# Attention's quarter blocks put next to each other, low words moved to VectorE, and another order at the head of the last layer

## The chip, the cores and the metric

The kernel runs on one core of a Trainium2 chip. The metric is the device time of one execution in microseconds (us), as the median of three runs. TensorE (PE) does the matmuls, VectorE (DVE), ScalarE (ACT) and GpSimd (POOL) the elementwise work, and SyncE (SP) issues nearly all the transfers.

## What is computed

Three layers follow each other. Attention is elementwise sigmoid attention over 4 batches of 12 heads, 448 tokens each, 64 wide. A router then assigns each of the 1792 tokens to one of 8 experts, by sorted preference and with a cap of 224, and each expert is a two-matmul block. A dense layer with a squared ReLU ends it.

```python
scores = scale * np.matmul(q, k.transpose(0, 1, 3, 2)) - np.log(S)
attn = 1.0 / (1.0 + np.exp(-scores)); x = np.matmul(attn, v)     # attention
out[mask] = np.maximum(x[mask] @ w1[e], 0.0) @ w2[e]             # per expert e
r = np.maximum(x @ w_in, 0.0); y = (s * (r * r) + b) @ w_out     # dense layer
```

Inputs are float32 (the dense layer's weights come as float64). Where full precision is wanted, a float32 operand is split in two words: a high word rounded to the matmul's format, and a low word that is the rest. Three matmuls of such words make one product.

## The kernel before

**Attention.** Heads come in pairs, pairs in groups of two. A group q (0 to 11) has seven blocks of scores: three blocks of 128 keys for each pair, and block 3, which holds the last 64 keys of both pairs. Block 3 is the two quarter blocks of the group: each of its matmuls uses a quarter of the array (64 rows, 64 columns), and four of them run at once, one in each quarter. The product with the values has the same shape there. The other score blocks use the array as two halves of 64 rows (two matmuls at once), the other value blocks as two halves of 64 columns.

The loop at line 453 runs over the groups. An iteration q has two halves. In a half, `split_qk` (line 277) splits one pair of q and k of group q + 2 on VectorE (lines 282 and 283); `values` (line 320) multiplies half of group q; `scores` (line 289) computes blocks of group q + 1; then `convert` turns one block of the dense layer's float64 weights to float32 on VectorE (lines 152 to 157) and issues its store (line 147) and the next load (line 141). The first half computes score blocks 0 to 2, the second blocks 3 to 6. In the second half `values` begins with the quarter blocks (line 328) and goes on with three full blocks (line 334). A sigmoid on ScalarE (line 313) takes a block of scores from PSUM to an `attn` tile; there are three PSUM buffers for scores.

At the top of an iteration SyncE issues the loads of two pairs of q and k (`load_qk`, lines 273 and 274) and of the values of group q + 2 (`load_v`, line 268). All of these and the conversions' transfers stand in SyncE's one queue in the order of the program, so that a load at the top of iteration q stands behind the transfers of the conversions of iteration q - 1. The values have three buffers; those of groups 0 and 1 are loaded ahead of the loop.

Every third iteration opens a batch (q = 3, 6, 9). It also computes the router's logits of the batch before: a matmul block in the first half (`gate`, line 354), and in the second half a turn of the logits (line 366), a copy to the tile L on ScalarE (line 376), and ranks on VectorE (`prefs`, lines 380 to 383). In the last batch, `bracket` takes the range of the logits in three stages (0 on VectorE, 1 with the matmul of line 393, 2 with that of line 401), each followed by small VectorE work.

In the last iterations the first four weight blocks of the experts are made ready: a transfer (`w_dma`), a high word on ScalarE (`w_high`, line 244) and at once its low word on GpSimd (`w_low(G)`, line 254). When attention ends, `prefs` of the last batch opens the router, a chain of small steps that go from engine to engine.

**Head of the last layer.** The dense layer's first product is done as a scheme of seven half-width products for each of 8 pairs of column blocks. `layer_mixed` (line 1125) writes out their order by hand as a list of (f, m): f is the block, m the product. A product is nine matmuls of 448 columns. Product (f, 3) accumulates in the same PSUM bank as (f, 5) and has to come after VectorE has taken (f, 5) out of it (line 1194). The weight blocks come in a list of units with an order of its own (line 218), and the products take them in that order; the copies of results go to scratch tiles chosen by the list `picks` (line 1146).

Of the kernel before, what the change touches and what calls it, by code (L numbers as in the profile page):

```python
# [8 lines left out]
F32 = mybir.dt.float32  # L9
# [10 lines left out]
B, H, S, D = 4, 12, 448, 64  # L20
# [26 lines left out]
NQ = B * NP // 2  # L47
# [18 lines left out]
def tile_kernel(ctx, tc, qT, kT, v, wg, w1, w2, wi, wo, s2, b2, cst, out):  # L66
    nc = tc.nc
    V, A, G, T = nc.vector, nc.scalar, nc.gpsimd, nc.tensor
# [55 lines left out]
    vp = att.enter_context(tc.tile_pool(name="vp", bufs=2))  # L124
    at = att.enter_context(tc.tile_pool(name="at", bufs=2))
# [33 lines left out]
    def convert():  # L159
        if not coming:  # L160
            return
        i = coming.pop(0)
        a = cgp.tile([128, 768], I32, name="co", bufs=3)
        b = cgp.tile([128, 768], I32, name="cb_", bufs=1)
        r = craw.pop(i)
        for step in range(3):
            to_float(a, b, r, step)
        if i < KG // 2:
            V.tensor_scalar(a, a, -(1 << 31), None, op0=ALU.bitwise_xor)
        cout.append((i, a))  # L170
        cv_out(1)
        cv_in()
# [33 lines left out]
    nu = {"dma": 0, "high": 0, "low": 0, "use": 0, "ahead": 5}  # L206
# [5 lines left out]
    for g in range(4):  # L212
        for e in (2 * g, 2 * g + 1):
            units += [w1[e, f] for f in range(KF)] + [w2[e, n] for n in range(KF)]
            where += [False] * (2 * KF)
        more = [narrow[f] for f in range(KG)] if g < 2 else []
        if g == 3:
            more = [(0, 1), (1, 1), (2, 1), (0, 2), (1, 2), (0, 3), (1, 3), (0, 4), (1, 4), (2, 2), (2, 3)]
            for f in range(3, KG // 2):
                more += [(f, 1), (f - 1, 4), (f, 2), (f, 3)]  # L220
            more += [(KG // 2 - 1, 4)]
        if g % 2:
            more += [w for of in products for w in of]
        units += more
        where += [False] * len(more)
# [22 lines left out]
    def w_low(eng=None):  # L248
        i = nu["low"]
        if i < nu["high"]:  # L250
            r, h = w_source(i), splits[i]
            lo = wlp.tile([128, KD, 128], F32R, name="wl")[:, :r.shape[1]]
            eng = eng or (G if where[i] else V)
            eng.tensor_sub(lo, r, h.bitcast(F32))  # L254
            splits[i] = (h, lo)
            nu["low"] += 1
# [6 lines left out]
    raw_qk, two_qk, vt, attn, pvs, plg, lgs, pts = {}, {}, {}, {}, {}, {}, {}, {}  # L263
    pairs = [(b, p) for b in range(B) for p in range(NP)]

    def load_v(q):
        vt[q] = vp.tile([128, 7, 128], F32, name="vt", bufs=3)
        nc.sync.dma_start(vt[q], v[q // 3, q % 3])

    def load_qk(i):  # L270
# [18 lines left out]
    def scores(q, units):  # L289
        if q >= NQ:  # L290
            return
        for r in units:
            p = ps_s.tile([128, 2, 512], F32, name="psc")
            if r == 3:
                work = [(2 * q + n, slice(HD, S), slice(n * 64, n * 64 + 64)) for n in range(2)]
            else:
                c = r % 4
                work = [(2 * q + r // 4, slice(c * 128, (c + 1) * 128), slice(0, 128))]
            plain = q < PLAIN or r == 3
            n_terms = 1 if plain else 3  # L300
            for m in range(n_terms):
                for j in range(2):
                    me = slice(j * D, (j + 1) * D)
                    for n, keys, rows in work:
                        if plain:
                            kx = qx = raw_qk[n]
                        else:
                            h, lo = two_qk[n]
                            kx, qx = ((h, h), (lo, h), (h, lo))[m]
                        T.matmul(p[rows, j, :S], kx[me, 1, keys], qx[me, 0], start=(m == 0),  # L310
                                 stop=(m == n_terms - 1), skip_group_check=True)
            attn[q, r] = at.tile([128, 2, S], F32, name="attn", bufs=7)
            A.activation(attn[q, r], p[:, :, :S], AF.Sigmoid, bias=nls, scale=1.0 / math.sqrt(D))  # L313
        if units[-1] == 6:
            for n in (2 * q, 2 * q + 1):
                raw_qk.pop(n)
                if q >= PLAIN:
                    two_qk.pop(n)
# [42 lines left out]
    def gate_turn(b, stop):  # L361
        lg = lgs.pop(b)
        pt = small_psum()
        pts[b] = pt[:CP, :NC * E].rearrange("p (c e) -> p c e", e=E)
        for c in range(NC):
            T.matmul(pts[b][:, c], lg[:, c * CP:(c + 1) * CP], ct[:, C_SEL:C_SEL + E], start=(c == 0),
                     stop=(stop and c == NC - 1))
# [18 lines left out]
    def bracket(stage):  # L386
        if stage == 0:
            lv = L[:, :NCH - NC].rearrange("p c e -> p (c e)")
            V.tensor_reduce(mm[:CP, 0:1], lv, axis=AX.X, op=ALU.max)
            V.tensor_reduce(mm[:CP, 1:2], lv, axis=AX.X, op=ALU.min, negate=True)  # L390
        elif stage == 1:
            pm = small_psum()
            T.transpose(pm[:2, :CP], mm[:CP], ident[:CP, :CP])
            m2 = ep.tile([2, 1], F32, name="m2")
            mt = ep.tile([2, CP], F32, name="mt")
            A.copy(mt, pm[:2, :CP])
            V.tensor_reduce(m2, mt, axis=AX.X, op=ALU.max)
            V.tensor_scalar(dg, ident[:2, :2], m2, None, op0=ALU.mult)
        else:
            pr = small_psum()  # L400
            T.matmul(pr[:, :2], on[:2], dg, start=True, stop=True)
            A.copy(mm, pr[:, :2])
            lb = ep.tile([128, 1], BF16, name="lb")
            V.tensor_add(mm[:, 0:1], mm[:, 0:1], mm[:, 1:2])
            V.scalar_tensor_tensor(lb, mm[:, 0:1], -MARGIN, mm[:, 1:2], op0=ALU.mult, op1=ALU.subtract)
            V.tensor_scalar(mm[:, 0:1], mm[:, 0:1], 1.77 * (1 + MARGIN) / LEVELS, None, op0=ALU.mult)
            V.tensor_scalar(mm[:, 0:1].bitcast(I32), mm[:, 0:1].bitcast(I32), 0x7F800000, None, op0=ALU.bitwise_and)
            V.tensor_scalar(least, mm[:, 0:1], LEVELS ** -7.0, None, op0=ALU.mult)
            V.tensor_copy(dv[0][:, 0:1], lb)
            V.tensor_copy(dv[0][:, 1:], mm[:, 0:1].to_broadcast([128, LEVELS]))  # L410
            V.tensor_scalar(th, kvec, dv[0][:, 1:2], dv[0][:, 0:1], op0=ALU.mult, op1=ALU.add)
# [18 lines left out]
    load_qk(2)  # L430
    load_qk(3)
    cv_in()
    load_v(1)
    cv_in()
    cv_in()
    scores(0, range(7))
# [16 lines left out]
    for q in range(NQ):  # L453
        b, t = divmod(q, 3)
        closing = b == B - 1
        for n in (2 * q + 5, 2 * q + 6):
            if n < 2 * NQ:
                load_qk(n)
        if q + 2 < NQ:
            load_v(q + 2)  # L460
        for half in range(2):
            if q + 2 < NQ:
                split_qk(2 * q + 4 + half)
            values(q, half)
            if t == 0 and b:
                if half:
                    gate_turn(b - 1, True)
                    prefs(b - 1)
                else:
                    gate(b - 1, 0, NP, NP)  # L470
                    gate_copy(b - 1)
            if closing and (t == 1 or t + half == 1):
                bracket(2 * t + half - 1)
            if closing and t == 2 and not half:
                gate(b, 0, NP - 2, NP - 2)
                gate_copy(b)
            scores(q + 1, range(3, 7) if half else range(3))
            n = 2 * (NQ - q) - half
            if 2 < n <= 6:
                w_dma()  # L480
            for _ in range({4: 1, 3: 1, 2: 2}.get(n, 0)):
                w_high()
                w_low(G)
            for _ in range(CONV[2 * q + half]):
                convert()
    gate_turn(B - 1, False)
    gate_last(B - 1)
    prefs(B - 1)
# [636 lines left out]
    def layer_mixed(y):  # L1125
        mov["b11"], mov["b21"] = y[:, :HK], y[:, HK:]
        half = slice(CAP, S)
# [15 lines left out]
        rest = [lambda: V.tensor_sub(mov["t4"][:, :, 1], srcs["t4"], mov["t4"][:, :, 0].bitcast(F32))]  # L1143
        tmps = [pool["y"].tile([128, S], F32, name="tmp", bufs=pool["tmp"]) for _ in range(3)]
        tmps += [late["rb"][:, n * S:(n + 1) * S] for n in range(3)]
        picks = [tmps[n] for n in (0, 1, 2, 3, 4, 5, 0, 1, 2, 3, 5)]
        tmps = [tmps[n] for n in (4, 0, 1, 2, 3, 5)]
        gn = gt[:, :, :, 64:64 + S]
        got, bank, tmp, held = {}, {}, {}, []
# [15 lines left out]
        def product(f, m):  # L1165
# [35 lines left out]
            if held and (f, m) in ((0, 7), (1, 7), (0, 6)):  # L1201
# [2 lines left out]
        nu["ahead"] = 4  # L1204
        n = KG // 2
        order = [(0, 1), (0, 2), (1, 1), (1, 2), (2, 1), (2, 2), (0, 7), (1, 7), (0, 6), (1, 6), (0, 4), (0, 5), (1, 4),
                 (0, 3), (1, 5), (1, 3), (2, 7), (2, 6), (2, 4), (2, 5)]
        for f in range(3, n - 1):
            order += [(f, 1), (f, 2), (f - 1, 3), (f, 7), (f, 6), (f, 4), (f, 5)]
        order += [(n - 1, 1), (n - 2, 3)] + [(n - 1, m) for m in (7, 6, 2, 5, 4, 3)]  # L1210
# [118 lines left out]
```

## Time and profile before

| what | value |
|---|---|
| median of three runs | 876.88 us (876.16 to 878.23) |
| the profiled execution's own time | 876.09 us |
| its span, from the first to the last instruction | 874.3 us |
| around the span | 1.8 us |
| PE busy | 857.2 us (98%) |
| DVE busy | 645.3 us (74%) |
| ACT busy | 509.9 us (58%) |
| POOL busy | 92.9 us (11%) |

The span is read in stretches: attention lasts until about 147 us, the router until about 184 us, the experts and the dense layer fill the rest. PE is busy nearly everywhere, so time is won or lost only where PE waits, where its matmuls are spaced wider than they need to be, or in the router's chain, where small steps wait for each other.

### The profile page before, as it was taken

What the parts mean: (1) busy time and instruction counts of PE and PEld (TensorE: products, weight loads), DVE (VectorE), ACT (ScalarE), POOL (GpSimd) and SP (SyncE); (2) the same over time, 40 slices, a digit from 0 to 9 for tenths busy, and PEclk for the clock granted to TensorE, in tenths of its full rate; (3) what the DMA queues carried; (4) which work ended last, traced back from release to release, by engine and by line L of the source; (5) the groups of instructions that cost most, each with busy time, mean ns of one, the idle gap of its engine ahead of it and who ended that gap; (6) DMA issues with size and microseconds to landing.
All of it is one profiled execution on the core that took longest, in us unless ns stands there. A gap on an engine that the chain in (4) does not pass through costs nothing.

```text
span 874.3 us, 14225 instructions
## 1 busy us (share of the span) xinstructions
PE 857.2 (98%) x5188; PEld 740.3 (85%) x5188; DVE 645.3 (74%) x1109; ACT 509.9 (58%) x887; POOL 92.9 (11%) x150
## 2 busy tenths in 40 slices
PE   9999999789999999999999999999999999999997
PEld 4444445579989999999999999999998999999997
DVE  2998979747778786789777957867897666866781
ACT  6666667736655576644665546766675555655440
POOL 1000003231000000000445330000000000000003
PEclk9999999969999999999999999999999999999999
DMA  8899995937669775668899986756743423333313
GB/s 307 312 335 363 352 346 178 288 94 263 217 200 324 252 262 178 220 209 297 282 330 323 284 250 206 250 191 202 230 144 106 127 90 118 119 99 95 104 35 131
DMA packets 76778, 190.40 MB, mean 218 GB/s; under 512 B 9120, under 2 KB 31136, under 8 KB 76448
## 3 DMA queue, kind: packets, MB, share of 16 engines
q1 hardware_dynamic: 68800, 164.28, 55.9%
q0 software_dynamic: 7904, 25.17, 10.2%
q8 instruction: 42, 0.69, 0.3%
q14 instruction: 32, 0.26, 0.1%
HBM read 161.11 MB, written 42.47 MB: 233 GB/s over the span
## 4 chain that ended last, share of the span: by engine, by line
PE 89%; DVE 5%; DMA 2%; ACT 1%; issue 1%; POOL 0%; POOLq 0%; DVEq 0%; ACTq 0%; SPq 0%
PE acc L757 15%; PE acc L758 7%; PE acc L1069 7%; PE acc L1072 7%; PE acc L1071 7%; PE psc L310 6%; PE pv L334 5%; PE acc L914 4%; PE acc L915 4%; PE acc L916 4%; PE acc L1178 4%; PE acc L1180 4%; PE acc L1179 4%; PE acc L783 1%; PE acc L784 1%; PE acc L785 1%
## 5 line engine op out<-in xcount | busy, mean ns | idle before, releaser
L244 ACT CAST wh<-raw 128x768 fp32r<-128x768 f32 (+1 forms) x248 | 201.2, 823 | 91.7 <-issue 66.5
L254 DVE TENSOR_TENSOR wl<-raw,wh 128x768 fp32r<-128x768 f32 (+1 forms) x244 | 225.8, 937 | 18.0 <-PE acc L1071 11.0
L757 PE MATMUL acc<-u,wh 128*128 128x448 f32 x384 | 120.8, 374 | 0.0
L758 PE MATMUL acc<-u,wl 128*128 128x224 f32 x384 | 101.6, 265 | 0.2 <-DVE wl L254 0.2
L757 PE MATMUL acc<-x,wh 128*128 128x448 f32 x288 | 94.9, 384 | 0.6 <-issue 0.6
L313 ACT ACTIVATE attn<-psc,nls 128x896 f32<-128x896 f32 x84 | 78.1, 1009 | 23.5 <-PE psc L310 23.4
L758 PE MATMUL acc<-x,wl 128*128 128x224 f32 x288 | 76.9, 267 | 0.0
L757 PEld LDWEIGHTS acc<-u,wh 128*128 128x128 f32 x384 | 72.1, 188 | 5.3
L758 PEld LDWEIGHTS acc<-u,wl 128*128 128x128 f32 x384 | 73.3, 191 | 0.4 <-DVE wl L254 0.4
L914 PE MATMUL acc<-y,wh 128*128 128x448 f32 x192 | 71.0, 370 | 0.7 <-ACT y L772 0.7
L915 PE MATMUL acc<-y,wh 128*128 128x448 f32 x192 | 70.3, 366 | 0.0
L916 PE MATMUL acc<-y,wl 128*128 128x448 f32 x192 | 70.2, 366 | 0.0
L762 ACT COPY tmp<-acc 128x224 f32<-128x224 f32 x96 | 32.9, 343 | 50.1 <-PE acc L758 49.8
L334 PE MATMUL pv<-attn,vt 128*64 128x448 f32 x288 | 59.4, 548 | 0.0
L757 PEld LDWEIGHTS acc<-x,wh 128*128 128x128 f32 x288 | 54.9, 191 | 4.8 <-issue 0.9
L1069 PE MATMUL acc<-wh,as 128*128 128x384 f32 x168 | 56.1, 334 | 0.0
L1071 PE MATMUL acc<-wl,as 128*128 128x384 f32 x168 | 56.1, 334 | 0.0
L1072 PE MATMUL acc<-wh,as 128*128 128x384 f32 x168 | 56.1, 334 | 0.0
L758 PEld LDWEIGHTS acc<-x,wl 128*128 128x128 f32 x288 | 55.8, 194 | 0.3 <-DVE wl L254 0.3
L763 DVE TENSOR_TENSOR tmp<-acc,tmp 128x224 f32<-128x224 f32 x78 | 30.1, 385 | 28.2 <-ACT tmp L762 27.9
L334 PEld LDWEIGHTS pv<-attn,vt 128*64 128x64 f32 x288 | 18.5, 136 | 34.8 <-issue 33.9
L648 POOL DMA_INDIRECT xr<-xs,idx x16 | 16.1, 1008 | 264.9 <-PE px L748 251.9
(339 smaller groups left out, 1985.8 us busy)
## 6 DMA issues: line engine op xcount, KB each, us to landing
raw<-in_w_dram SPq DMA_DIRECT2D x128, 384.0 KB, 3.7
raw<-nw SPq DMA_DIRECT2D x64, 384.0 KB, 3.7
craw<-in_wi_dram SPq DMA_DIRECT2D x16, 768.0 KB, 7.3
raw<-mx SPq DMA_DIRECT2D x32, 384.0 KB, 4.9
nw<-co SPq DMA_DIRECT2D x24, 384.0 KB, 7.5
craw<-in_wo_dram SPq DMA_DIRECT2D x8, 768.0 KB, 7.2
ra<-in_wo_dram SPq DMA_DIRECT2D x8, 768.0 KB, 5.1
hs<-nw POOLq DMA_DIRECT2D x16, 384.0 KB, 9.9
```

Source lines behind the costliest of these rows:

```text
L244: A.copy(h, r)
L254: eng.tensor_sub(lo, r, h.bitcast(F32))
L313: A.activation(attn[q, r], p[:, :, :S], AF.Sigmoid, bias=nls, scale=1.0 / math.sqrt(D))
L334: T.matmul(pv[j * 64:(j + 1) * 64, :S], v[:, 4 * block + c, j * D:(j + 1) * D], a[:, j], start=(block == 0 and c == 0), stop=(block == 1 a ...
L757: T.matmul(p[:, :2 * CAP], wh, src[:, k].rearrange("p a s -> p (a s)"), start=(k == 0), stop=False)
L758: T.matmul(p[:, :CAP], wl, src[:, k, 0], start=False, stop=(k == n - 1))
L914: T.matmul(p, wh, src[:, k, 0], start=first, stop=False)
L915: T.matmul(p, wh, src[:, k, 1], start=False, stop=False)
L916: T.matmul(p, wl, src[:, k, 0], start=False, stop=last)
L1069: T.matmul(acc, hi, wh[:, cols], start=(opens[j] and u == 0 and c == 0), stop=False, skip_group_check=True)
L1071: T.matmul(acc, hi, wl[:, cols], start=False, stop=False, skip_group_check=True)
L1072: T.matmul(acc, lo, wh[:, cols], start=False, stop=(u == 3 and c == 1), skip_group_check=True)
```

## The change

- In an iteration of attention the first half now computes score blocks 0 to 3 and the second blocks 4 to 6. So block 3 of group q + 1 is the last thing that TensorE does in the first half, and the quarter blocks of the values of group q are the first in the second. The `attn` tiles have 8 buffers instead of 7.
- The values have 2 buffers instead of 3. The load of group 1 ahead of the loop is taken out, and iteration q loads the values of group q + 1 instead of q + 2, at the same place in SyncE's queue.
- Stages 1 and 2 of `bracket` come half an iteration later.
- The low words of the first four weight blocks are made on VectorE instead of GpSimd, after the conversion of that half.
- At the head of the last layer product (2, 7) comes ahead of (1, 3), which stood right behind (1, 5); the units (2, 2) and (1, 4) change places, and so do two entries of `picks`.

```diff
-            more = [(0, 1), (1, 1), (2, 1), (0, 2), (1, 2), (0, 3), (1, 3), (0, 4), (1, 4), (2, 2), (2, 3)]
+            more = [(0, 1), (1, 1), (2, 1), (0, 2), (1, 2), (0, 3), (1, 3), (0, 4), (2, 2), (1, 4), (2, 3)]
...
-        vt[q] = vp.tile([128, 7, 128], F32, name="vt", bufs=3)
+        vt[q] = vp.tile([128, 7, 128], F32, name="vt", bufs=2)
...
-            attn[q, r] = at.tile([128, 2, S], F32, name="attn", bufs=7)
+            attn[q, r] = at.tile([128, 2, S], F32, name="attn", bufs=8)
...
     cv_in()
-    load_v(1)
     cv_in()
...
-        if q + 2 < NQ:
-            load_v(q + 2)
+        if q + 1 < NQ:
+            load_v(q + 1)
...
-            if closing and (t == 1 or t + half == 1):
-                bracket(2 * t + half - 1)
+            if closing and 1 <= 2 * t + half <= 4 and 2 * t + half != 2:
+                bracket((2 * t + half) // 2)
...
-            scores(q + 1, range(3, 7) if half else range(3))
+            scores(q + 1, range(4, 7) if half else range(4))
...
                 w_high()
-                w_low(G)
             for _ in range(CONV[2 * q + half]):
                 convert()
+            while nu["low"] < nu["high"]:
+                w_low()
...
-        picks = [tmps[n] for n in (0, 1, 2, 3, 4, 5, 0, 1, 2, 3, 5)]
+        picks = [tmps[n] for n in (0, 1, 2, 3, 4, 5, 0, 1, 3, 2, 5)]
...
-                 (0, 3), (1, 5), (1, 3), (2, 7), (2, 6), (2, 4), (2, 5)]
+                 (0, 3), (1, 5), (2, 7), (1, 3), (2, 6), (2, 4), (2, 5)]
```

## Rows read from the trace of the kernel before

**Rows 1.** Busy time by engine, 75 to 100 us; after POOL: granted clock, DMA share, GB/s
```profile
75.00:100.00 25.00, 25.00 (x184) 11.67 (x180) 21.44 (x32) 16.16 (x21) 0.00 (x0) 1.00 0.96 353
```
**Rows 2.** Timeline of PE, one plain iteration (q = 8): start, duration, engine, line, work
```profile
102.39 2.48 PE L334 MATMUL pv<-attn,vt 128*64 128x448 f32 x12
104.80 0.47 PE L310 MATMUL psc<-wh 64*128 64x448 f32 x2
...
106.81 0.98 PE L328 MATMUL pv<-attn,vt 64*64 64x448 f32 x8
107.73 2.48 PE L334 MATMUL pv<-attn,vt 128*64 128x448 f32 x12
110.13 0.98 PE L310 MATMUL psc<-rqk 64*64 64x448 f32 x8
...
113.14 0.60 PE L334 MATMUL pv<-attn,vt 128*64 128x448 f32 x2
```
**Rows 3.** Timeline of PE: iterations 1, 10 and 11 begin; the matmul of line 393
```profile
22.08 1.35 PE L334 MATMUL pv<-attn,vt 128*64 128x448 f32 x6
...
126.39 2.48 PE L334 MATMUL pv<-attn,vt 128*64 128x448 f32 x12
129.17 0.26 PE L393 MATMUL psc<-ident,mm 112*2 112x112 f32 x1 [0.31 <-DVE mm L390]
138.01 2.48 PE L334 MATMUL pv<-attn,vt 128*64 128x448 f32 x12
```
**Rows 4.** Timeline of SyncE's queue: value loads issued in iterations 0, 2, 5, 7
```profile
19.43 0.96 SPq L268 DMA_DIRECT2D vt<-in_v_dram  x1
...
42.12 0.64 SPq L268 DMA_DIRECT2D vt<-in_v_dram  x1
...
77.39 0.66 SPq L268 DMA_DIRECT2D vt<-in_v_dram  x1
...
99.12 0.42 SPq L268 DMA_DIRECT2D vt<-in_v_dram  x1
```
**Rows 5.** DMA issues, the same four loads: KB, us from issue to landing
```profile
vt<-in_v_dram SPq DMA_DIRECT2D x1, 448.0 KB, 6.7
vt<-in_v_dram SPq DMA_DIRECT2D x1, 448.0 KB, 7.5
vt<-in_v_dram SPq DMA_DIRECT2D x1, 448.0 KB, 7.7
vt<-in_v_dram SPq DMA_DIRECT2D x1, 448.0 KB, 7.2
```
**Rows 6.** Timelines of ACT and DVE: L copied (iteration 3), ranks begin (iterations 3, 6)
```profile
53.95 0.19 ACT L376 COPY L<-psc 112x32 f32<-112x32 f32 x1 [0.34 <-PE psc L366]
...
59.11 0.42 DVE L380 TENSOR_TENSOR ge<-L 112x256 f32<-112x256 f32 x1
...
93.72 0.42 DVE L380 TENSOR_TENSOR ge<-L 112x256 f32<-112x256 f32 x1
```
**Rows 7.** Timelines of DVE, POOL and ACT at the end of attention
```profile
139.72 0.96 DVE L157 CUSTOM_DVE_ANT_0 co<-co,cb__1657 128x1536 uint16<-128x1536 uint16 x1
140.65 6.75 POOL L254 TENSOR_TENSOR wl<-raw,wh 128x768 fp32r<-128x768 f32 x3 [4.88 <-ACT wh L244]
145.77 2.45 DVE L157 CUSTOM_DVE_ANT_0 co<-co,cb__1686 128x1536 uint16<-128x1536 uint16 x1
147.19 0.19 ACT L376 COPY L<-psc 112x32 f32<-112x32 f32 x1 [1.85 <-PE psc L372]
148.14 0.41 DVE L380 TENSOR_TENSOR ge<-L 112x256 f32<-112x256 f32 x1
```
**Rows 8.** Timeline of PE, head of the last layer: the first matmul of product (1, 3)
```profile
676.10 0.44 PE L1178 MATMUL acc<-x,wh 128*128 128x448 f32 x1 [1.75 <-DVE rb L1194]
```
**Rows 9.** Busy time by engine around the router's end, columns as in rows 1
```profile
177.50:191.00 13.50, 11.49 (x47) 8.45 (x47) 2.94 (x11) 1.76 (x4) 4.01 (x4) 0.50 0.38 107
191.00:200.00 9.00, 9.00 (x61) 8.63 (x60) 6.97 (x15) 7.38 (x16) 5.20 (x16) 1.00 0.43 152
```

## Prediction

> **What bounds the kernel now.** I read the busy time by stretches first. In attention PE has no idle time that counts, VectorE is at 86% and the DMA engines at 96% [rows 1]: three resources near their limit at once. PE sets the pace only as long as what it reads has arrived, and the change moves one such arrival, that of the values. So the next view is SyncE's queue beside PE's timeline. A plain iteration takes 10.75 us on PE [rows 2], one that opens a batch 13.25 [rows 2, 3], and iteration 1 begins at 22.08 [rows 3]. Iterations 3 and 6 then begin at about 43.6 and 78.3, iteration 8 at 102.39 [rows 2]. SyncE issues the value load of an iteration far behind the point at which PE begins that iteration: at 42.12 for iteration 2, which PE began at 32.8, and at 77.39 for iteration 5, which PE began at 67.6 [rows 3, 4]. Nothing suffers from that today, since those values are wanted two iterations later. Outside attention the views to read are the chain at its end [rows 7] and the one long wait of PE at the head of the last layer [rows 8].
>
> **Quarter blocks side by side.** Nothing is computed more or less. Two blocks of the same array shape now follow each other, so one change of shape per iteration goes. A full block of values has six passes of PE (twelve matmuls, two at once) in 2.40 us, 0.40 a pass; the quarter block of values has two passes (eight, four at once) in 0.92, 0.46 a pass [rows 2]. If all of that excess hangs on the change of shape, a merge saves 0.12; a pass bare of any change would be shorter than 0.40, so up to 0.2 is possible, and if the excess belongs to the pass, nothing. I take 0.15, in eleven iterations 1.65 us, bounds 0 to 2.2. The moved score block needs its PSUM buffer back from the sigmoid of block 0. That is the fourth block of a half as now, so I cost it at nothing.
>
> **Values one iteration later.** The load keeps its place in SyncE's queue but serves the next iteration. The new wait stands on PE at the first matmul of an iteration; behind it are queued all its score blocks, and ScalarE's sigmoids wait for those. SyncE's own wait (for the buffer of group q - 1) is the one it has now. The only gain is that 448 KB go from ahead of the loop, which at 353 GB/s [rows 1] pulls the transfers and VectorE's work behind them some 1.3 us forward.
> Iteration 1: the load issued at 19.43 lands 6.7 later [rows 4, 5], at 26.1, or 24.8 with the 1.3 off. PE is there at 22.08 less 0.15: it stands for 2.9 us.
> Iteration 3: its values ride on the load of 42.12, which lands after 7.5, at 49.6, now 48.3. PE would come at 24.8 + 2 x 10.6 = 46.0, so by then it has stood another 2.3.
> Here PE's delay comes back through VectorE. The ranks of iteration 3 need L. Before, L was there at 54.14 [rows 6], 10.6 after PE began the iteration; a quarter block of scores (0.92 less 0.15) now comes ahead of it, so 11.3. That makes 48.3 + 11.3 = 59.6. VectorE, in order, came to the ranks at 59.11 [rows 6] and would now be there at 57.8. It stands until 59.6, so it loses its lead and is 0.5 later than before. Behind it are queued the conversions, and behind these SyncE's loads.
> Iteration 6: the load of 77.39, 0.5 later, landing after 7.7, gives 85.6. PE would come at 48.3 + 13.1 + 2 x 10.6 = 82.6 and stands for 3.0. L follows at 96.9, where the ranks began at 93.72 [rows 6], so VectorE and SyncE are 3.2 late.
> Iteration 8: 99.12 + 3.2 + 7.2 = 109.5; PE would come at 85.6 + 13.1 + 10.6 = 109.3. It begins at 109.5 instead of 102.39, 7.1 late. After that PE's own pace rules: iteration 10 begins at 109.5 + 10.6 + 13.1 = 133.2 (before 126.39 [rows 3]). The merges before iteration 8 are lost in the waits; only those after it count.
>
> **Bracket and low words.** PE's wait of 0.31 for the first stage [rows 3] goes, since the matmul comes half an iteration later; the small VectorE steps keep their number. The end of attention is read from the ranks: L was written by 147.38, yet they began at 148.14 [rows 7], because VectorE was still converting. A conversion step that took 0.96 took 2.45 while GpSimd made low words (three in 6.75) [rows 7]. With these on VectorE the slow steps go, but four low words are added to it, queued behind the conversion and ahead of the ranks. By the slowed step alone (1.5 us, at least three of its kind in that stretch) the trade comes out at zero or better. I take it that the ranks begin when L is there, a gain of 0.76; if not, that gain is missing, and up to 1 us is lost. From the start of iteration 10 to L it was 147.38 - 126.39 = 21.0, now less 0.15 and 0.31: 20.5. So L comes at 153.7 where the ranks began at 148.14: the router starts 5.6 us later.
>
> **Head of the layer.** PE stands 1.75 us at product (1, 3) until VectorE has added (1, 5) out of the bank [rows 8]. With (2, 7) between them, nine matmuls cover that: the next product begins at once, and the add was over before 676.1. The exchange of units makes one low word early that is twice as wide; VectorE has room for it, and both are wanted at 674 or later. I take 1.75 as the gain, bounds 1.0 to 2.0.
>
> **Sum.** 5.6 - 1.75 = 3.85 later, 879.9 against the profiled execution's 876.09. The median of the runs lies 0.8 above that execution, so I predict 880.7.
>
> **Rivals.**
> A, the forecast: values late, and VectorE held by the ranks. 880.7, with its bounds 878.5 to 883.
> B, values late, but the chain of VectorE and SyncE isn't held back. Then iteration 6 gets its values at 77.39 - 1.3 + 7.7 = 83.8 and iteration 8 begins at 83.8 + 23.7 = 107.5. The router starts 3.6 later, and the time is 878.7. For it: ranks are short. Against it: VectorE works in order and has no second path to L.
> C, faster: the values are there in time all along. Its place is the start of iterations 1 to 8, and it decides if the first load lands within some 3 us of its issue instead of 6.7, so that 21.9 holds. Then L comes at 147.38 - 1.65 - 0.31 = 145.4 and the ranks with it, 2.7 earlier, and with the 1.75 the time is 872.4. For it: SyncE may issue earlier with one load fewer ahead of it. Against it: four loads took 6.7 to 7.7 [rows 5] at a DMA share of 0.96 [rows 1].
> D, the clock falls while PE stands. It is at half from 177.5 to 191 and back at full after that [rows 9], where PE had small matmuls and waits before. If the stand of 3 us at iteration 6 is followed by the same 13.5, some 10.5 of work at half clock loses 5.3, which gives 886.0; at iteration 1 the later waits swallow 2.3 of it, which gives 883.7. Against it: the head of the last layer had 1.75 of idle [rows 8] without a long aftermath. [...]
>
> **Chances.** A 0.50, B 0.13, C 0.14, D 0.18, and 0.05 for anything else. About 0.2% (1.75 us) is what a measurement can tell from no change, so the same is 875.1 to 878.6. Slower: A, D and half of B, 0.75. Faster: C and a little, 0.15. Same: half of B and the rest, 0.10. For the range I leave C out at the bottom and little at the top: 876.0 to 886.0.
>
> **What would show it.** Right: PE's first matmul of iterations 1, 3 and 6 waits for a DMA of vt, 2 to 3 us each; the ranks of iterations 3 and 6 wait for L; the ranks of the last batch begin at about 153.7, right behind L; line 254 has no POOL rows in attention; product (1, 3) has no wait. Wrong: no PE wait for vt in attention (C), or rows at half clock before 147 us (D). If the router starts 5.6 later but the end is not 3.9 later, the head of the layer or the router's clock was mis-sized.

## The result, and the profile after

The changed kernel takes 881.87 us (median of 22 runs, 877.1 to 884.8), the kernel before 875.81 in the same runs. The ratio is 1.0052 with a 95% interval of 1.0038 to 1.0066: 4.6 us slower. (The two medians are 6.1 apart, the means of the same runs 4.65; the ratio is close to that of the means.) The profiled execution took 882.63 us with a span of 880.8, which is 6.5 us over the one before (874.3). Single executions of either kernel lie up to 3 to 6 us from the median, so sizes in one trace and in the medians are told apart below.

The page after, its first lines: busy time by engine, the granted clock in 40 slices, and the group of the value matmuls with its idle time.

```profile
PE 856.3 (97%) x5188; PEld 746.9 (85%) x5188; DVE 642.6 (73%) x1113; ACT 509.4 (58%) x887; POOL 85.0 (10%) x146
...
PEclk9899999999999999999999999999999999999999
...
L334 PE MATMUL pv<-attn,vt 128*64 128x448 f32 x288 | 62.9, 574 | 8.5 <-DMA vt<-in_v_dram 8.5
```

PE does the same matmuls, and 8.5 us of idle time stand ahead of line 334 where there were none. The granted clock, the row PEclk, has a dent in the second slice that the page before hadn't. PE's timeline shows where (iterations 1, 3 and 6 begin; in brackets the idle time and what ended it):

```profile
26.26 3.25 PE L334 MATMUL pv<-attn,vt 128*64 128x448 f32 x8 [4.64 <-DMA vt<-in_v_dram]
...
50.47 0.97 PE L334 MATMUL pv<-attn,vt 128*64 128x448 f32 x4 [0.38 <-DMA vt<-in_v_dram]
...
88.29 2.18 PE L334 MATMUL pv<-attn,vt 128*64 128x448 f32 x8 [3.31 <-DMA vt<-in_v_dram]
```

SyncE issued the loads behind the first and the last wait at these points, and they landed after 6.9 and 7.2 us, as long as the loads in [rows 5] took:

```profile
19.19 0.33 SPq L268 DMA_DIRECT2D vt<-in_v_dram  x1
...
80.95 0.55 SPq L268 DMA_DIRECT2D vt<-in_v_dram  x1
...
vt<-in_v_dram SPq DMA_DIRECT2D x1, 448.0 KB, 6.9
vt<-in_v_dram SPq DMA_DIRECT2D x1, 448.0 KB, 7.2
```

VectorE's ranks in iterations 3 and 6 and at the end of attention, with the copy of L on ScalarE ahead of the last (to be held against [rows 6, 7]):

```profile
61.92 0.43 DVE L380 TENSOR_TENSOR ge<-L 112x256 f32<-112x256 f32 x1 [1.66 <-ACT L L376]
...
101.39 0.42 DVE L380 TENSOR_TENSOR ge<-L 112x256 f32<-112x256 f32 x1 [3.95 <-ACT L L376]
...
157.81 0.19 ACT L376 COPY L<-psc 112x32 f32<-112x32 f32 x1 [1.85 <-PE psc L372]
158.03 0.43 DVE L380 TENSOR_TENSOR ge<-L 112x256 f32<-112x256 f32 x1 [0.35 <-ACT L L376]
```

VectorE now stands for L, 1.7 and 4.0 us, where it was late before. The last ranks follow L at once, but at 158.03 instead of 148.14: attention ends 9.9 us later. And the clock, by stretches (granted clock, DMA share and GB/s are the last three numbers):

```profile
24.60:31.40 6.80, 5.14 (x14) 1.84 (x16) 6.59 (x10) 0.00 (x0) 0.00 (x0) 0.50 0.69 260
31.50:89.00 57.50, 53.82 (x392) 28.54 (x390) 49.19 (x72) 38.06 (x47) 0.00 (x0) 1.00 0.91 328
89.40:92.80 3.40, 3.40 (x16) 0.97 (x14) 3.30 (x6) 0.00 (x0) 0.00 (x0) 0.50 0.92 333
```

About each of the two long waits the granted clock is 0.50 instead of 1.00; at the first it fell at 24.6 us, while PE still stood (until 26.26), at the second at 89.4, 1.1 us after PE had begun again. From the last ranks on, the time is won back in part. The stretch from there to the first expert matmul is 1.0 longer, the experts and the dense layer up to the head of the last layer 1.4 shorter, the head 2.9 shorter (102.8 instead of 105.7 from its first matmul to the end of its last), the rest equal. 9.9 + 1.0 - 1.4 - 2.9 = 6.6, the difference of the two spans up to rounding. Of the 2.9, some 1.3 is not the edit's (last section); what the 1.0 and the 1.4 come from is not shown.

### The profile page after: what moved, and what is told of

Read it like the earlier page. It is cut to its first block, busy times and chain, and to the rows that moved or that the text cites. A ratio compares the mean times of both kernels' runs of the same rounds, so it can differ in the third digit from the quotient of the medians.

```text
span 880.8 us, 14238 instructions
## 1 busy us (share of the span) xinstructions
PE 856.3 (97%) x5188; PEld 746.9 (85%) x5188; DVE 642.6 (73%) x1113; ACT 509.4 (58%) x887; POOL 85.0 (10%) x146
## 4 chain that ended last, share of the span: by engine, by line
PE 89%; DMA 5%; DVE 2%; ACT 1%; issue 1%; SPq 1%; POOL 0%; POOLq 0%; DVEq 0%; ACTq 0%
PE acc L757 16%; PE acc L758 8%; PE acc L1072 7%; PE acc L1071 7%; PE acc L1069 7%; PE pv L334 6%; PE psc L310 5%; PE acc L915 4%; PE acc L914 4%; PE acc L916 4%; PE acc L1178 4%; PE acc L1180 4%; PE acc L1179 4%; DMA vt<-in_v_dram 3%; PE acc L783 1%; PE acc L784 1%
## 5 line engine op out<-in xcount | busy, mean ns | idle before, releaser
L254 DVE TENSOR_TENSOR wl<-raw,wh 128x768 fp32r<-128x768 f32 (+1 forms) x248 | 229.5, 937 | 21.3 <-PE acc L1071 11.3
L334 PE MATMUL pv<-attn,vt 128*64 128x448 f32 x288 | 62.9, 574 | 8.5 <-DMA vt<-in_v_dram 8.5
```

The costliest lines, as they stand in the source:

```text
L334: T.matmul(pv[j * 64:(j + 1) * 64, :S], v[:, 4 * block + c, j * D:(j + 1) * D], a[:, j], start=(block == 0 and c == 0), stop=(block == 1 a ...
```

## Experiments: one part at a time

Four kernels take the change apart. The first has the value loads alone:

```diff
-        vt[q] = vp.tile([128, 7, 128], F32, name="vt", bufs=3)
+        vt[q] = vp.tile([128, 7, 128], F32, name="vt", bufs=2)
...
-    load_v(1)
...
-        if q + 2 < NQ:
-            load_v(q + 2)
+        if q + 1 < NQ:
+            load_v(q + 1)
```

> The kernel before with only the value loads changed: two buffers, the values of group q + 1 loaded in iteration q. Theory V (the loss is the late values alone; the other parts gain 4 to 5 us together): PE waits for vt at iterations 1 and 6, 3 to 5 us each, the ranks of the last batch begin 9 to 11 us later than before, the time is 8 to 10 us longer, ratio 1.009 to 1.011. Rival O (the loss comes from four score blocks in the first half, with three PSUM buffers for them): no loss here, ratio 1.000, and no wait for vt over 1 us.

Measured: 881.37 us, ratio 1.0059 (1.0041 to 1.0078), 5.1 us slower. PE's timeline:

```profile
24.58 0.60 PE L334 MATMUL pv<-attn,vt 128*64 128x448 f32 x2 [2.35 <-DMA vt<-in_v_dram]
...
37.71 1.02 PE L334 MATMUL pv<-attn,vt 128*64 128x448 f32 x2 [2.30 <-DMA vt<-in_v_dram]
...
86.33 0.60 PE L334 MATMUL pv<-attn,vt 128*64 128x448 f32 x2 [1.26 <-DMA vt<-in_v_dram]
```

The late values alone give a loss as large as that of the whole change, so theory V holds against O. Its sizes were too high: 1.3 to 2.4 us a wait instead of 3 to 5, the last ranks 6.8 later instead of 9 to 11, and a time 5.1 longer instead of 8 to 10. The wait of iteration 2, the middle row, was not expected.

The second is the changed kernel with the value loads put back as they were (three buffers fit beside the eight of `attn`):

> The changed kernel with the value loads of the kernel before: three buffers, the values of group q + 2 loaded in iteration q, those of group 1 ahead of the loop. Theory V: no PE wait for vt, the last ranks begin at about 145.4 instead of 148.1, the time is 872, ratio 0.995 (0.993 to 0.997). Rival O: PE still waits in attention, on the sigmoids before the quarter blocks, and the time is not below that of the kernel before, ratio 1.000 or more.

Measured: 871.11 us (6 runs), ratio 0.9933 (0.9908 to 0.9958): 5.2 us faster than the kernel before by the medians, the fastest version here. PE waits for no values; the last ranks begin at 145.80, expected 145.4:

```profile
101.44 2.48 PE L334 MATMUL pv<-attn,vt 128*64 128x448 f32 x12
...
112.10 1.35 PE L334 MATMUL pv<-attn,vt 128*64 128x448 f32 x6
...
145.80 0.42 DVE L380 TENSOR_TENSOR ge<-L 112x256 f32<-112x256 f32 x1 [0.39 <-ACT L L376]
```

The plain iteration between the first two rows takes 10.66 us instead of 10.75 [rows 2].

The third has the order at the head of the last layer alone (the first and the last two edits of the diff above):

> The kernel before with only the order at the head of the last layer changed. The step of the prediction: the wait of 1.75 us at product (1, 3) is gone and no other takes its place, the time is 1.75 us shorter, ratio 0.998. Rival: VectorE's work is late anyway and the wait turns up at (2, 6) or (2, 4), ratio 1.000.

Measured: 873.98 us, ratio 0.9970 (0.9943 to 0.9997), 2.3 us faster. Where the first matmul of product (1, 3) waited 1.75 [rows 8], it waits 0.16, and no other wait came in this layer's head, which got 1.6 us shorter in the trace (104.1 instead of 105.7):

```profile
678.22 0.45 PE L1178 MATMUL acc<-x,wh 128*128 128x448 f32 x1 [0.16 <-DVE rb L1194]
```

The fourth has the low words alone:

```diff
                 w_high()
-                w_low(G)
             for _ in range(CONV[2 * q + half]):
                 convert()
+            while nu["low"] < nu["high"]:
+                w_low()
```

> The kernel before with only the first four low words moved from GpSimd to VectorE. The step of the prediction: the conversion steps of 2.2 to 2.5 us take 0.55 to 0.96 again, the last ranks begin right behind L, 0.7 us earlier, ratio 0.999. Rival: the four low words, 0.95 each and queued ahead of the ranks, hold them, and they begin at 148.1 or later, ratio 1.000 or more.

Measured: 875.73 us, ratio 0.9986 (0.9966 to 1.0005): the size fits, the timing alone doesn't settle it. The trace does:

```profile
143.58 0.96 DVE L157 CUSTOM_DVE_ANT_0 co<-co,cb__1682 128x1536 uint16<-128x1536 uint16 x1
144.46 1.82 DVE L254 TENSOR_TENSOR wl<-raw,wh 128x768 fp32r<-128x768 f32 x2
147.56 0.42 DVE L380 TENSOR_TENSOR ge<-L 112x256 f32<-112x256 f32 x1 [1.28 <-ACT L L376]
```

The last conversion step took 0.96 instead of 2.45 [rows 7], and VectorE, with the four low words on it, stood 1.28 us for L and began the ranks 0.6 sooner.

## Experiments: what the quarter blocks give by themselves

> The kernel before with only the quarter blocks put next to each other (score block 3 in the first half, 8 buffers for attn; three buffers and the old place for the values). The step of the prediction: 0.15 us for each of eleven iterations; a plain iteration takes 10.6 us instead of 10.75, the last ranks begin 1 to 1.7 us sooner, ratio 0.998. Rival O: the fourth score block of the first half waits for a PSUM buffer, a plain iteration takes 10.75 or more, ratio 1.000 or more. A third case: PE is sooner, but VectorE's conversions end attention as before, so the ranks begin at 148 all the same and the ratio is 1.000.

```diff
-            attn[q, r] = at.tile([128, 2, S], F32, name="attn", bufs=7)
+            attn[q, r] = at.tile([128, 2, S], F32, name="attn", bufs=8)
...
-            scores(q + 1, range(3, 7) if half else range(3))
+            scores(q + 1, range(4, 7) if half else range(4))
```

Measured: 877.36 us, ratio 1.0013 (0.9995 to 1.0031): no gain, where 0.998 was expected, though most plain iterations took 10.62 to 10.66. The profiled execution is the slowest of the twelve (881.25), so its trace shows what can go wrong and not what is typical. In it PE's transpose for `bracket` waits 3.49 us for VectorE, which at that point comes from the ranks; the prediction had priced this wait at 0.31 [rows 3]:

```profile
127.20 2.48 PE L334 MATMUL pv<-attn,vt 128*64 128x448 f32 x12
...
131.61 0.42 DVE L380 TENSOR_TENSOR ge<-L 112x256 f32<-112x256 f32 x1
...
132.77 0.24 DVE L390 TENSOR_REDUCE mm<-L 112x1 f32<-112x96 f32 x1
...
133.16 0.26 PE L393 MATMUL psc<-ident,mm 112*2 112x112 f32 x1 [3.49 <-DVE mm L390]
```

It is VectorE that came late there, not PE that came early. Iteration 10 began at 127.20, where it had begun at 126.39 [rows 3], but the ranks began 4.0 us later than in the kernel before:

```profile
127.62 0.42 DVE L380 TENSOR_TENSOR ge<-L 112x256 f32<-112x256 f32 x1
```

Ahead of them VectorE had stood 1.88, 1.70 and 1.55 us for loads of q and k. PE had stood for such a load too, and iteration 8 took 12.04 us: score block 3 reads both pairs of its group, so in the first half it wants the second pair half an iteration sooner, a cost that the prediction did not ask about. Behind the 3.49 us the granted clock was 0.50 for 3.4 us (134.0 to 137.4), and the last ranks began at 153.40 instead of 148.14. Whether such late loads took the gain in the other eleven executions is not shown.

So the same with the bracket's edit of the change added:

> The kernel with only the quarter blocks put next to each other, and the bracket's stages 1 and 2 half an iteration later as well. If the 3.5 us that PE stood at line 393 ate the gain of the quarter blocks, no wait over 0.4 us is left there and the time falls below that of the kernel before, ratio 0.997 to 0.999; PE ends attention 1.5 us sooner, and the ranks wait for VectorE's conversions. If the wait only moves on (to line 401, or to VectorE's end of attention), the ratio stays at 1.000 to 1.002.

Measured: 875.99 us against 877.99 of the kernel before in these runs, ratio 0.9987 (0.9966 to 1.0008). The wait is gone, PE is done 1.9 us sooner (L at 145.43 instead of 147.38), and VectorE's conversions set the end, as they did before [rows 7]:

```profile
145.25 0.18 ACT L376 COPY L<-psc 112x32 f32<-112x32 f32 x1 [1.85 <-PE psc L372]
146.29 0.96 DVE L157 CUSTOM_DVE_ANT_0 co<-co,cb__1686 128x1536 uint16<-128x1536 uint16 x1
147.17 0.42 DVE L380 TENSOR_TENSOR ge<-L 112x256 f32<-112x256 f32 x1
```

The intervals of the two overlap, so the times show no gain of the bracket's edit, and the trace does not show one either. In this execution VectorE had ended the step that line 393 waits for at 127.2, and PE was through the first values of iteration 10, behind which that matmul stood before the edit, at 127.4. So there would have been no long wait without the edit either:

```profile
126.92 0.24 DVE L390 TENSOR_REDUCE mm<-L 112x1 f32<-112x96 f32 x1
```

## Experiments: how late values grow to twice their price

In the changed kernel the late values cost 881.87 against 871.11, some 10.4 us by the two ratios; in the kernel before they cost 5.1. Six kernels look for what the 10.4 are made of. The first two change where the load stands. In one, it is issued in the second half of the iteration, behind the matmuls that free its buffer, and group 1 is again loaded ahead of the loop:

```diff
     cv_in()
+    load_v(1)
     cv_in()
...
-        if q + 1 < NQ:
-            load_v(q + 1)
...
             values(q, half)
+            if half and q + 2 < NQ:
+                load_v(q + 2)
```

> The changed kernel, still with two buffers for the values, but the load of group q + 2 is issued in the second half of iteration q, right behind the matmuls that free its buffer and ahead of that half's conversion; group 1 is loaded ahead of the loop. Theory V (only the place of the load in SyncE's queue counts, not the number of buffers): the loads come some 6 us sooner, land at about the point where PE wants them, PE waits at most 1 us for any, and the time is 871 to 874 (ratio 0.993 to 0.998). Rival (two buffers are too few wherever the load stands, since it has to wait for PE to free one): waits of 2 us and more stay, the time is 878 or more.

Measured: 875.00 us, ratio 0.9990 (0.9964 to 1.0015). By the ratios about half of the loss is gone with two buffers as well (5.4 us), and 5.0 are missing to the three buffers. So the place in the queue is a large part of the loss but not all; neither theory's time came (871 to 874, or 878 and more). One long wait is left, where two conversions stand in the half ahead of the load; it was issued at 72.62, 10.7 us after PE had begun that half:

```profile
72.62 0.84 SPq L268 DMA_DIRECT2D vt<-in_v_dram  x1
...
80.76 0.97 PE L334 MATMUL pv<-attn,vt 128*64 128x448 f32 x4 [2.69 <-DMA vt<-in_v_dram]
```

In the other, the load moves ahead of the four loads of q and k at the top of the iteration:

> The changed kernel with the load of values ahead of the four loads of q and k in each iteration instead of behind them: a small dose of what the earlier place gives. Theory V: each load is issued some 2 us sooner, the first wait falls from 4.6 to about 3 us and that of iteration 6 to about 1.5, and the time is 2 to 5 us shorter, 877 to 880. Rival (the DMA engines are full, so what is issued sooner lands no sooner, or q and k come late instead and VectorE waits): 881 to 883.

Measured: 879.58 us, ratio 1.0033 (1.0012 to 1.0053). The first wait fell as expected, the one of iteration 6 didn't:

```profile
11.88 0.33 SPq L268 DMA_DIRECT2D vt<-in_v_dram  x1
...
23.71 0.60 PE L334 MATMUL pv<-attn,vt 128*64 128x448 f32 x2 [2.99 <-DMA vt<-in_v_dram]
...
85.28 1.08 PE L334 MATMUL pv<-attn,vt 128*64 128x448 f32 x4 [3.24 <-DMA vt<-in_v_dram]
```

The first load was issued 7.3 us sooner (11.88 instead of 19.19), far more than the 2 expected, but PE had its values only 2.6 sooner: this load took some 11.8 us instead of 6.9. Issued sooner, it did not land sooner by as much. The time is 2.3 us shorter by the medians and 1.7 by the ratios, with overlapping intervals, so a gain is not shown.

The next puts the way back through VectorE to the test:

```diff
-                    prefs(b - 1)
+                    prefs(b - 1, 2 if closing else 0)
...
+            if t == 1 and b and not closing and not half:
+                prefs(b - 1, 1)
```

(The second argument splits `prefs`: 0 is the copy of L alone, 1 the ranks alone, 2 both.)

> The changed kernel with VectorE's ranks of iterations 3 and 6 put half an iteration later, behind the next conversion; all of the work stays. Theory A of the prediction (PE's delay comes back through VectorE, which stands at the ranks until L is there, and so delays conversions, SyncE and the next values): VectorE stands for L in neither iteration, the wait for the values of iteration 6 falls from 3.3 to about 1 us, the last ranks begin 3 us sooner or more, the time is 877 to 879. Theory B (no such way back): the waits for vt stay as they are and the time is 881 to 883.

Measured: 878.27 us, ratio 1.0014 (0.9992 to 1.0035), 3.6 us less than the change by the medians and 3.3 by the ratios. VectorE stands for L in neither iteration, and the wait of iteration 6 fell from 3.31 to 1.15, as theory A said. Behind that shorter wait the granted clock stayed at 1.00, so the gain holds the half clock of iteration 6 as well:

```profile
68.86 0.42 DVE L383 TENSOR_TENSOR ge<-L 112x256 f32<-112x256 f32 x1
...
84.33 0.97 PE L334 MATMUL pv<-attn,vt 128*64 128x448 f32 x4 [1.15 <-DMA vt<-in_v_dram]
```

The next puts the half clock to the test:

```diff
+            if q in (1, 6) and not half:
+                keep_clock(14, small_psum()[:CP])
             values(q, half)
```

> The changed kernel with 14 matmuls of zeros (3 us at full clock) ahead of the values of iterations 1 and 6, where PE stands; they end before the values land and write to a buffer that nobody reads. Theory D (the clock falls because PE stands, and this adds to the delay): no half clock between 20 and 100 us, iteration 1 takes 10.6 to 11 us instead of 13.1, the time is 2 to 4 us shorter, 878 to 880. Rival (the delay is set by the landing of later values, and a PE at full clock only stands longer): iterations 2, 3 and 6 wait for vt longer by as much as the clock gives, and the time is within 1 us of 881.9.

Measured: 880.18 us, ratio 1.0034 (1.0014 to 1.0055). The granted clock stayed at 1.00:

```profile
24.60:31.40 6.80, 5.34 (x40) 3.04 (x44) 6.59 (x11) 1.95 (x3) 0.00 (x0) 1.00 0.77 287
31.50:100.00 68.50, 67.40 (x479) 35.19 (x473) 57.55 (x84) 43.03 (x55) 0.00 (x0) 1.00 0.92 331
```

Iteration 1 took 11.0 us instead of 13.1, iteration 6 began 2.1 sooner (at 86.20), and the last ranks began at 154.29, 3.7 sooner. The time fell by 1.7, less than either the trace or the expectation says, and with overlapping intervals.

Both edits together:

> The changed kernel with both: the ranks of iterations 3 and 6 half an iteration later, and 14 matmuls of zeros ahead of the values of iterations 1 and 6. If the way back through VectorE and the half clock are separate prices, the gains of the two runs before (3.6 and 1.7 us) add up: about 876.5, and what is left over the kernel with early values (871.1) is the lateness of the loads alone, some 5 us. If they are one price seen twice (each lets PE come sooner and only stand longer), the time stays at that of the better one, 878 to 879.

Measured: 879.81 us, ratio 1.0048 (1.0030 to 1.0066), which read as one price seen twice. But the zeros had themselves become the delay: the values of iteration 6 had landed at 83.3 (issued at 76.8, 6.5 to land), and PE worked on zeros from 82.96 to 86.1. So once more, with zeros ahead of iteration 1 alone:

> As the kernel with both edits, but the matmuls of zeros stand ahead of iteration 1 alone. In the run with both, the values of iteration 6 had landed at 83.3 us, while PE worked on zeros until 86.0: if these zeros ate the gain, iteration 6 begins at 83 to 84, the last ranks begin some 2.5 us sooner (151 to 152), and the time is 876.5 to 877.5, so that the half clock and the way back through VectorE do add up. If the gains are one price seen twice, the time stays at 879 to 880.

Measured: 877.15 us, ratio 1.0009 (0.9983 to 1.0036). The time is the expected one, though by the ratios it is only 0.4 us below that of the later ranks alone. Its trace is not the expected one: iteration 6 does begin without a wait, but this execution had its long wait at iteration 3, with half clock behind it (four value matmuls took 1.76 us, where four took 0.97 in the row of the later ranks above), and the last ranks began at 153.93, not at 151 to 152:

```profile
49.80 1.76 PE L334 MATMUL pv<-attn,vt 128*64 128x448 f32 x4 [2.72 <-DMA vt<-in_v_dram]
```

What follows: the way back through VectorE is shown, at 3.3 to 3.6 us with the half clock that it brings about at iteration 6. The half clock behind the waits is shown in the traces (a granted clock of 0.50 for 6.8 and 3.4 us in that of the changed kernel); by the medians it is worth 1 to 2 us, within the uncertainty. Whether the two add up isn't settled. Nor is why the late values cost twice as much here as in the kernel before: no run took these parts out of that one. The one trace of the late values alone has less of each: 5.9 us of waits for values against 8.5, VectorE's stands for L at iterations 3 and 6 of 0.95 and 1.94 against 1.66 and 3.95, and half clock for 3.4 us against 10.2 ahead of 100 us.

## Why the prediction was right, point by point

- **The values.** Right in kind and place: waits at iterations 1 and 6 of 2.9 and 3.0 foreseen, 4.64 and 3.31 seen. Iteration 3 began 6.9 us after 43.58 where 4.7 was foreseen, and stood only 0.38, since iteration 1 had already lost time to the half clock. The 1.3 us by which the transfers were to come forward were missing in this pair of traces: the first load was issued at 19.19 where the load in its place had been issued at 19.43, and landed at 26.1 as that one had. Over the other traces the term is borne out. With the load at this place, the six kernels with two buffers issued it at 18.1 to 19.3, the six with three at 19.4 to 21.2, which is 1.5 sooner on average.
- **The way back through VectorE.** Right, against rival B: the ranks waited for L at the two places foreseen, and putting them off gave 3.3 to 3.6 us. It was too small at iteration 6, where VectorE stood 3.95 us and the ranks began at 101.39 instead of 96.9.
- **The clock.** Rival D was given as an alternative to the forecast; it came on top of it. About the stands of 4.64 and 3.31 us the granted clock was 0.50 for 6.8 and 3.4 us. D's price, worked out from a stretch of 13.5 us, was too high. The last ranks came 4.3 us later than forecast (158.0 against 153.7). Of these, 2.7 were there when iteration 6 began (88.29 against 85.6), and 1.7 are the half clock in it (14.79 us instead of 13.1). The 2.7 go back to loads: that of iteration 3 was issued at 42.00 and landed after 8.3 us, where 40.8 and 7.5 were forecast, and the delay went on through L and VectorE. The half clock of iteration 1 (13.1 us instead of 10.6) left little by itself in this trace, as D had said for that place: at iteration 3 PE still stood for its values.
- **Quarter blocks.** 0.15 us an iteration was taken, 0.09 to 0.12 measured. As foreseen, what they gave before iteration 8 was lost in the waits. What the moved score block costs was put at nothing, with a look at its PSUM buffer alone; that it wants q and k sooner was left out, and alone the quarter blocks gave no gain.
- **Bracket.** Priced at the 0.31 of the trace before. With the merges this gave 20.5 from the start of iteration 10 to L, and 20.48 was measured (137.52 to 158.00), the same as with the values put back. The 3.49 of the quarter blocks alone came from a late VectorE, in one execution.
- **Low words.** Right: no row of GpSimd in attention, the slow steps gone, the ranks behind L at once.
- **Head of the layer.** 1.75 was taken; the wait went from 1.75 to 0.16, and the time fell by 2.3 us with this edit alone. In the traces the edit shortens the head by 1.6 us; what the changed kernel's head gained above that, 1.3, isn't the edit's (last section).
- **Rival C** gave 872.4 for values in time; the kernel that has them takes 871.11. So the sum of the other parts, 4.5, was right to 0.7 us by the medians (5.2) and to 1.4 by the ratio (5.9, interval 3.7 to 8.1).

The mechanism of the forecast was right, and by the ratio so was its size, 4.6 us against 3.85. That the number came so near was luck in part, because errors met: in the trace attention ended 4.3 later than forecast, and the head of the layer gave 1.2 more back, by a pace that the edit does not decide.

## What to carry to other kernels

A load's lead is not counted in iterations of the engine that uses it but from the point where its queue issues it: here the queue stood up to 10 us behind PE because it shared the order with slower work, and one buffer less used up the whole lead. A wait that another engine's work hangs on can come back through that engine, as it did here through VectorE (3.3 to 3.6 us). Before a wait that has grown is put down to the engine that got faster, look which of the two moved: the 0.31 us became 3.49 because VectorE came 4 us late, while PE was no earlier. When work is moved forward, ask of all that it reads when it lands. And parts that pay by themselves are worth testing without the part that makes room for them: here the room was there anyway.

## What the runs showed of the hardware that was not expected

In attention, the first value matmuls behind a stand ran at about half pace in some places and not in others. Two took 1.02 us behind a stand of 2.30 (iteration 2 of the values alone), but 0.60 behind one of 2.35 (iteration 1 there). Four took 1.76 behind one of 2.72 (zeros ahead of iteration 1 alone), but 0.97 behind one of 2.69 (the load in the second half) and behind the 3.31 of the changed kernel, where the clock fell only after them. Over these stands the length by itself doesn't decide the pace at which PE begins again.

At the head of the last layer matmuls of 448 columns follow each other at 202 ns in some executions and at 206 in others, with the granted clock at 1.00 in both. These are stretches of 50 us of the kernel before and of the changed one:

```profile
690.00:740.00 50.00, 50.00 (x243) 45.41 (x242) 32.59 (x48) 26.23 (x43) 0.00 (x0) 1.00 0.34 105
...
695.00:745.00 50.00, 50.00 (x248) 46.35 (x247) 32.11 (x47) 26.61 (x44) 0.00 (x0) 1.00 0.38 111
```

243 against 248 matmuls, 2%. Over the head of the layer, from its first matmul to the end of its last, each pace and each order has its own time, to within 0.02 us over all 14 traces:

| order at the head | pace 206 ns | pace 202 ns |
|---|---|---|
| as before | 105.7 us (4 kernels) | 104.4 us (values alone) |
| changed | 104.1 us (3 kernels) | 102.8 us (6 kernels) |

So the order is worth 1.6 us at either pace and the pace 1.3 in either order, and the order does not decide the pace. The cause of the pace stays open.
